# Half of the input transposes as DMA transposes, a re-ordered front and two filler groups in a hand-ordered spectral-plus-MLP kernel

## The chip, the core and the metric

The kernel runs on one core of a Trainium2 chip. A core has a matrix engine (PE; its weight loads are listed apart as PEld), three engines for elementwise work (VectorE or DVE, ScalarE or ACT, GpSimd or POOL), a queue engine that issues DMAs (SyncE or SP; ACT issues some too), and 16 DMA engines that carry them out. Each engine runs its own list of instructions strictly in order and waits on semaphores for the others. The metric is the device time of one execution in microseconds (us).

## The reference, cut to what matters

```python
x = A_x                                                       # 2048 x 512
g = sigmoid((x * gate_w).sum(-1))
a = irfft2(rfft2(x) * (w_r + 1j*w_i))                         # over both axes
h = x @ w1 + b1                                               # 2048 x 1792
b = (h * tanh(softplus(h))) @ w2                              # 2048 x 512
out = g * a + (1 - g) * b
```

Both branches read the same x. B_x is not used.

## The kernel before

**Tiles.** The 2048 rows of x are 16 tiles of 128 rows, t = 0 to 15, and four chunks c of four tiles. The 1792 columns of the hidden layer are 14 blocks ft.

**The MLP branch.** It wants x with its 512 columns on partitions (xT). For this `tr{t}` (PE, four 128x128 transposes against an identity matrix, L547) writes a PSUM bank, and `evx{t}` (ACT or DVE) copies it into xT. `m{c}_{ft}` is a group of four 128x512 matmuls (L791), `h{c}_{ft}` its Mish activation on ACT (L795), `n{t}_0` the second layer for a tile: 14 matmuls of 128x512 (L818).

**The spectral branch.** It goes through stages of 64 small matmuls each, with a copy out of PSUM after each pair: `bf` (sum and difference of the halves of x's columns, DVE, L560), `p` (L570, with the p matrix RF, loaded by `cRF`) and `ep`, `d` (L584) and `ed`, then eight DMAs `sh` that regroup y1 into In (`sh0_*` need d0 to d7 and ed0 to ed3, `sh1_*` the rest), then `t` (L669, with the tables M, loaded by `ldM0` to `ldM3`) and `et`, the filter on DVE (`p2`, `p1`, `ad`, L682 to L690, eight blocks q), an edge correction `e1`, `e2`, `e3` that needs all blocks, then `it` (L743, all of which need e3), the DMAs `hx`, `id` (L767), `ey` and `ip` (L802). `s` and `o` combine both branches, and `out` stores them.

**The filter matrices.** W_r and W_i come by ten DMAs (`wr0s0` to `wi1s1`), and sixteen copies of 32 partitions by 2064 elements (`wrm...`, `wim...`, L626 to L634) spread them out. `win`, `wrn`, `wc` and `wz` finish them.

**The gate.** `gt0` to `gt15` on DVE (L592) multiply x with gate_w, which `gwl` loads, `gwb` (PE) spreads over partitions and `gwe` copies to SBUF.

**What sets the order.** One string, ORDER, names every task once, as `name:engine:slot`. `place` splits it into one list for each engine, and the slot is the PSUM bank (or temporary buffer) that the task's result takes; a task that takes a bank waits for the last readers of what was in it. `emit` turns dependences into semaphore waits. Nothing is reordered at run time, so a task that waits holds all that stands behind it on its engine. An issuing engine likewise holds the DMAs that stand behind a waiting one.

**What the change touches.** XTP is the number of tiles that PE transposes; a tile above it gets `xt{t}`, one DMA from x in HBM to xT with `transpose=True`, issued by SP (L462, L530). NWARM is the number of 128x256 matmuls on a constant that PE runs before x has arrived (`warm`, L488). FILL gives the sizes of groups `fl{k}` of 128x128 matmuls on a constant (L498), whose result is never read. `tab` (L505) is a one-element Mish activation.

Of the kernel before, what the change touches and what calls it, by code (L numbers as in the profile page):

```python
# [301 lines left out]
w1_0:sp x4:sp w1_4:sp x8:sp warm:pe:0 tr0:pe:0 tr1:pe:1 tr2:pe:2 w1_9:sp  # L302
x12:sp wr0s2:sp wi1s1:sp wr1s1:sp wr1s0:sp cFD:sp wr0s0:sp bf0_1:dve bf0_0:dve
evx0:dve wi1s0:sp wr0s1:sp wi0s2:sp wi0s1:sp wi0s0:sp bf2_1:dve ldM1:sp tr3:pe:0
gwb:pe:3 evx1:act bf2_0:dve evx2:act p2:pe:4 p3:pe p0:pe:6 tr_b:pe:2 evx3:dve
gwe:dve p1:pe ep0:act ep2:act ev_b:dve m0_0:pe:2 h0_0:act m0_2:pe:6 m0_1:pe:7
# [7 lines left out]
p13:pe p15:pe gt9:dve gt10:dve ep14:act p8:pe:6 m0_13:pe:4 tr14:pe:5 p9:pe
ep12:act gt11:dve m0_12:pe:0 ep8:act gt12:dve evx14:dve h0_12:act tr12:pe:5 tr13:pe:2
evx12:dve evx13:dve h0_13:act m0_10:pe:3 d4:pe:0 d5:pe ed2:act m1_10:pe:2 h1_10:act
d6:pe:4 d12:pe:6 d13:pe ed6:act d7:pe d14:pe:0 h0_10:act d15:pe m1_13:pe:2
h1_13:act d0:pe:6 d1:pe ed0:act gt13:dve wrm110:dve ed3:dve m0_7:pe:3 d2:pe:4
d3:pe ed1:act m1_12:pe:2 m0_5:pe:6 sh0_2:sp sh0_1:sp ed7:act h0_5:act tr15:pe:4
evx15:act m0_11:pe:5 gt14:dve gt15:dve sh0_0:sp wip1:pool wip0:pool h0_11:act wim010:dve  # L320
# [36 lines left out]
ip0:pe:0 s15_384:dve ip2:pe:2 s2:dve out3:act s13_0:dve s0:dve out13:sp out15_384:sp
out1:act n10_0:pe:5 s10_0:dve s11_0:dve out11:act n15_0:pe:0 s15_0:dve out15_0:act
"""


def _build(nc, A_x, A_w_r, A_w_i, B_x, B_w1, B_b1, B_w2, gate_w, out, XTP=16, LATE=8, NWARM=14,
           W1P=((0, 4), (4, 9), (9, 14)), XP=((0, 2), (2, 4), (4, 8), (8, 12), (12, 16)), SH=2):
    cs = _build_consts()
    d_front = nc.inline_tensor(_bf16_bits(cs["front"]), name="c_front").bitcast(BF)
# [7 lines left out]
    with es:  # L373
        def sb(name, shape, dt):
            return es.enter_context(nc.sbuf_tensor(name, shape, dt))
# [116 lines left out]
        def filler(k, n):  # L492
            fb = _Buf("b1")

            def f_fill(e):
                ins = None
                for _ in range(n):
                    ins = e.matmul(bank(fb)[:, 0:128], one, one, start=True, stop=True)  # L498
                return ins

            G.add(f"fl{k}", "fill", dict(pe=f_fill), ("pe", n, 128), writes=[fb])

        for k_, n_ in enumerate(FILL):
            filler(k_, n_)
# [86 lines left out]
        for t in range(NT):  # L591
            t_gt.append(dve(f"gt{t}", "gate", "stt", 512, lambda e, t=t: e.scalar_tensor_tensor(  # L592
                out=junk, in0=x_sb[:, t, :], scalar=1.0, in1=gwr, op0=ALU.mult, op1=ALU.mult, accum_out=zc[:, t:t + 1]), lock=True,
# [21 lines left out]
        for ri, (dstv, nm) in enumerate(((Wr, "wr"), (Wi, "wi"))):  # L615
            dp = t_bf + t_tr[:XTP] + t_gt if ri else []
            sv = wsr if ri == 0 else wsi
            for fh in range(2):
# [33 lines left out]
                else:  # L652
                    dve(f"{nm}n{fh}", "wm", "dup", 4160, f_dup, lock=True, reads=mv, writes=[wk])
                G.add(f"{nm}c{fh}", "wm", {g: (lambda e, sv=sv, dstv=dstv, f0=f0: e.tensor_copy(
                    out=sv[:, :, f0:f0 + 32].rearrange("p c f -> p f c"), in_=dstv[:, f0:f0 + 32, 0:129:128])) for g in ("dve",)}, ("wc", 64),
# [192 lines left out]
def bass_gated_mix__spectral_gfnet__dense_activation_mish__prompt_kernel(  # L848
    nc: bass.Bass,
    A_x: bass.AP,  # L850
    A_w_r: bass.AP,
    A_w_i: bass.AP,
    B_x: bass.AP,
    B_w1: bass.AP,
    B_b1: bass.AP,
    B_w2: bass.AP,
    gate_w: bass.AP,
    out: bass.AP,
):
    _build(nc, A_x, A_w_r, A_w_i, B_x, B_w1, B_b1, B_w2, gate_w, out)  # L860
# [28 lines left out]
```

## Time and profile before

| | us |
|---|---|
| median of 3 runs | 134.41 (133.45 to 135.21) |
| the profiled execution | 133.68 |
| its span in the profile | 132.4 |
| PE busy / DVE busy / ACT busy in the span | 126.2 / 96.8 / 71.2 |

The profiled execution is longer than its span by 1.3 us, which lie around the program. A PE instruction in the profile is shown from its start to its modelled end, so neighbours overlap: what one takes from the path is the distance between starts, which the chain of waits shows (four 128x128 matmuls in 0.22 us, four of 128x512 in 0.86 us). In a row of the profile, `out<-in` are the names of the SBUF tensors: rA holds x and later W_i, rB the output of bf and later the table G, rX holds xT and later the output, rE holds In, rF the tables M, rS the raw W rows, `ps` is PSUM.

### The profile page before, as it was taken

The numbers are of one execution on the slowest core, as the hardware profiler recorded it, in microseconds if no ns is written. First come the engines' busy times: TensorE is split into PE (matmuls) and PEld (weight loads), VectorE is DVE, ScalarE is ACT, GpSimd is POOL, SyncE is SP. The second block draws the span as 40 slices with busy tenths as digits, with TensorE's granted clock in tenths as the row PEclk, the third lists the DMA queues.
The fourth block names the chain that finished last, engine by engine and source line by source line (L and its number), as shares of the span: only waits on it lengthen the run. The fifth ranks groups of instructions, "written<-read, shape, count | busy, mean of one in ns | idle before, by whom it ended". The sixth has DMA issues, their size and how long they took to land.

```text
span 132.4 us, 2194 instructions
## 1 busy us (share of the span) xinstructions
PE 126.2 (95%) x871; PEld 69.5 (52%) x886; DVE 96.8 (73%) x171; ACT 71.2 (54%) x104; POOL 7.4 (6%) x12
## 2 busy tenths in 40 slices
PE   7796999999999999999999999999999999999992
PEld 5453755766644544655444556744555555455451
DVE  0697898767499999999999616770099597947872
ACT  3469898999979696998770285302122312230000
POOL 3000000000200970000000000000000000000000
PEclk9999999999999999999999999999999999999999
DMA  3799999960387879993397000009800000201463
GB/s 114 227 330 404 219 195 190 202 155 7 139 287 215 236 242 229 269 351 106 87 309 282 0 0 0 5 0 335 309 0 0 5 0 0 79 0 45 161 248 109
DMA packets 12392, 20.16 MB, mean 152 GB/s; under 512 B 1437, under 2 KB 7326, under 8 KB 12318
## 3 DMA queue, kind: packets, MB, share of 16 engines
q1 hardware_dynamic: 11056, 18.05, 47.8%
q10 hardware_dynamic: 1326, 1.97, 4.1%
q8 instruction: 7, 0.11, 0.4%
q14 instruction: 3, 0.02, 0.1%
HBM read 12.66 MB, written 2.10 MB: 111 GB/s over the span
## 4 chain that ended last, share of the span: by engine, by line
PE 89%; DMA 3%; ACT 2%; DVE 2%; issue 1%; SPq 0%
PE ps L818 36%; PE ps L791 34%; DMA rA<-in_A_x_dram 3%; PE ps L570 3%; PE ps L669 3%; PE ps L743 3%; PE ps L584 3%; PE ps L767 3%; PE ps L547 3%; PE ps L802 2%; DVE rX L812 2%; ACT L795 1%; ACT rC L475 1%; ACT hs L795 1%; SPq L463 0%
## 5 line engine op out<-in xcount | busy, mean ns | idle before, releaser
L791 PE MATMUL ps<-rX,w_sb 128*128 128x512 bf16 x216 | 52.2, 379 | 0.6
L791 PEld LDWEIGHTS ps<-rX,w_sb 128*128 128x128 bf16 x224 | 20.4, 98 | 20.5 <-ACT rC L475 0.9
L818 PE MATMUL ps<-w_sb,hs 128*128 128x512 bf16 x109 | 24.7, 379 | 0.2
L795 ACT ACTIVATE hs<-ps,b1f 128x512 bf16<-128x512 f32 x28 | 18.2, 697 | 3.0 <-PE ps L791 2.8
L777 DVE TENSOR_TENSOR rA<-tmp,ps 128x512 bf16<-128x512 f32 x16 | 10.4, 682 | 11.4 <-ACT tmp L475 11.3
L818 PEld LDWEIGHTS ps<-w_sb,hs 128*128 128x128 bf16 x112 | 10.8, 98 | 12.4
L475 ACT ACTIVATE rC<-ps 128x1024 bf16<-128x1024 f32 x13 | 13.0, 1026 | 2.4 <-PE ps L669 1.2
L795 ACT ACTIVATE rS<-ps,b1f 128x512 bf16<-128x512 f32 x14 | 9.3, 699 | 7.2 <-PE ps L791 6.9
L818 PE MATMUL ps<-w_sb,rS 128*128 128x512 bf16 (+2 forms) x68 | 12.7, 335 | 0.1
L818 PE MATMUL ps<-w_sb,rD 128*128 128x512 bf16 x56 | 12.7, 379 | 0.0
L592 DVE SCALAR_TENSOR_TENSOR w_sb<-rA,w_sb 128x512 bf16<-128x512 bf16 x16 | 11.0, 688 | 0.3
L682 DVE TENSOR_TENSOR tmp<-rC,rA 64x1024 bf16<-64x1024 bf16 x16 | 10.6, 684 | 0.4
L795 ACT ACTIVATE rD<-ps,b1f 128x512 bf16<-128x512 f32 x14 | 9.2, 697 | 1.5 <-PE ps L791 1.5
L818 PEld LDWEIGHTS ps<-w_sb,rS 128*128 128x128 bf16 x70 | 6.2, 98 | 5.5
L818 PEld LDWEIGHTS ps<-w_sb,rD 128*128 128x128 bf16 x56 | 5.4, 97 | 6.5 <-DVE rX L808 0.2
L560 DVE TENSOR_TENSOR rB<-rA 128x1024 bf16<-128x1024 bf16 (+1 forms) x10 | 5.4, 578 | 4.5 <-DMA rA<-in_A_x_dram 4.5
L812 DVE SCALAR_TENSOR_TENSOR rX<-ps,omg,rX 128x512 bf16<-128x512 f32 (+2 forms) x9 | 6.1, 687 | 3.0 <-PE ps L818 2.9
L807 ACT ACTIVATE rX<-ps,omg 128x512 bf16<-128x512 f32 x5 | 3.5, 691 | 8.7 <-PE ps L818 8.7
L475 ACT ACTIVATE tmp<-ps 128x512 f32<-128x512 f32 x5 | 2.9, 594 | 9.7 <-PE ps L767 9.7
L547 PE MATMUL ps<-identt,rA 128*128 128x128 bf16 x64 | 5.5, 222 | 2.0 <-ACT omg L505 1.1
L475 ACT ACTIVATE rD<-ps 128x1024 bf16<-128x1024 f32 x7 | 7.1, 1025 | 0.3 <-PE ps L584 0.2
L475 DVE CAST rF<-ps 128x1024 bf16<-128x1024 f32 x5 | 5.8, 1218 | 1.2 <-PE ps L743 1.0
(72 smaller groups left out, 134.4 us busy)
## 6 DMA issues: line engine op xcount, KB each, us to landing
w_sb<-in_B_w_dram SPq DMA_DIRECT2D x4, 640.0 KB, 8.4
rF<-c_m SPq DMA_DIRECT2D x4, 512.0 KB, 5.2
rE<-rD SPq DMA_DIRECT2D x8, 256.0 KB, 3.5
rB<-c_g SPq DMA_DIRECT2D x4, 512.0 KB, 6.2
rC<-rF SPq DMA_DIRECT2D x7, 256.0 KB, 3.0
rA<-in_A_x_dram SPq DMA_DIRECT2D x3, 512.0 KB, 9.7
out_dram<-rX ACTq DMA_DIRECT2D x6, 256.0 KB, 2.1
rW<-rW SPq DMA_DIRECT2D x4, 260.0 KB, 3.5
```

The lines of the kernel that those rows point to most:

```text
L475: fns = dict(dve=lambda e: e.tensor_copy(out=o(), in_=i()), act=lambda e: e.activation(o(), i(), AF.Copy))
L547: ins = e.transpose(bankb(b)[:, 128 * dt_:128 * (dt_ + 1)], x_sb[:, t, 128 * dt_:128 * (dt_ + 1)], identt[:, :])
L560: return e.tensor_tensor(out=xu[:, a:b_, uv, :], in0=x_sb[:, a:b_, 0:256], in1=x_sb[:, a:b_, 256:512], op=ALU.add if uv == 0 else ALU.subt ...
L570: ins = e.matmul(bank(b, i)[:, 128 * c:128 * (c + 1)], xu[:, t, c // 2, c % 2:256:2], RF, start=True, stop=True)
L584: ins = e.matmul(o[:, 2 * e_:2 * e_ + 2, uv, :], zu[:, c, g, :], FD[:, c, :].rearrange("p (r k) -> p r k", r=2), start=True, stop=True)
L592: t_gt.append(dve(f"gt{t}", "gate", "stt", 512, lambda e, t=t: e.scalar_tensor_tensor(out=junk, in0=x_sb[:, t, :], scalar=1.0, in1=gwr, op ...
L682: return e.tensor_tensor(out=zv(z)[lo], in0=Y[hi, f0:f0 + 8, :], in1=Wi[hi, f0:f0 + 8, 0:128], op=ALU.mult)
L777: return e.tensor_tensor(out=yb[:, t:t + 2, 256 * h:256 * h + 256].rearrange("p t (i e) -> p t i e", e=2), in0=t4(z), in1=o4(bank(b, 1)), ...
L791: ins = e.matmul(bank(b), w1_sb[:, dt_, 128 * ft:128 * (ft + 1)], xT[:, c, dt_, :, :], start=(dt_ == 0), stop=(dt_ == 3))
L795: G.add(f"h{c}_{ft}", "mish", dict(act=lambda e, c=c, ft=ft, b=b: e.activation(hs[c][:, ft, :], bank(b), AF.Mish, bias=b1f[:, ft:ft + 1])) ...
L812: dve(name, "fin", "psums", hi - lo, lambda e: e.scalar_tensor_tensor(out=bs[:, t, lo:hi], in0=bank(b)[:, 0:hi - lo], scalar=col[:, t:t + ...
L818: ins = e.matmul(bank(b)[:, 0:hi - lo], hs[c][:, ft, 128 * tl:128 * (tl + 1)], w2_sb[:, ft, lo:hi], start=(ft == 0), stop=(ft == NFT - 1))
```

## The change

The code of the tasks stays; three numbers and the order string change.

```diff
-FILL = ()
+FILL = (3, 9, )
 ORDER = """
-cRF:act braw:act ebase:pool ones:pool ident:pool wrp0:pool x0:sp x2:sp gwl:act
+wrp1:pool ones:pool gwl:act x0:sp wrp0:pool ident:pool warm:pe:0 tr0:pe:0 tr1:pe:1
...
-def _build(..., XTP=16, LATE=8, NWARM=14,
+def _build(..., XTP=8, LATE=8, NWARM=13,
```

With XTP=8, `tr8` to `tr15` and `evx8` to `evx15` are gone, and `xt8` to `xt15` take their place on SP's queue. The new order moves nearly every task. What the prediction speaks of:

**SP's queue after the last piece of x.** Before, these rows follow it: all ten W loads, the d matrix (`cFD`, c_front) and one M table.

```order
L463 DMA rS<-in_A_w_r_dram 16x257
L463 DMA rS<-in_A_w_i_dram 16x32x257
L463 DMA rS<-in_A_w_r_dram 16x32x257
L463 DMA rS<-in_A_w_r_dram 16x8224
L463 DMA w_sb<-c_front 128x512
L463 DMA rS<-in_A_w_r_dram 16x8224
L463 DMA rS<-in_A_w_i_dram 16x8224
L463 DMA rS<-in_A_w_r_dram 16x31x257
L463 DMA rS<-in_A_w_i_dram 16x257
L463 DMA rS<-in_A_w_i_dram 16x31x257
L463 DMA rS<-in_A_w_i_dram 16x8224
L463 DMA rF<-c_m 128x2048
```

In the changed kernel the same place holds three W_r pieces, two M tables, cFD and the eight transposes; behind them come `sh0_*` (rE<-rD x4) and the W_i pieces.

```order
L463 DMA rS<-in_A_w_r_dram 16x8224
L463 DMA rF<-c_m 128x2048
L463 DMA rS<-in_A_w_r_dram 16x257
L463 DMA w_sb<-c_front 128x512
L463 DMA rS<-in_A_w_r_dram 16x31x257
L463 DMA rF<-c_m 128x2048
L462 DMA_TRANSPOSE rX<-in_A_x_dram 128x4x128 x8
L463 DMA rE<-rD 128x1x1024 x4
L463 DMA rS<-in_A_w_i_dram 16x8224
L463 DMA rE<-rD 128x1x1024
L463 DMA rS<-in_A_w_i_dram 16x32x257
L463 DMA rS<-in_A_w_i_dram 16x257
```

So seven of the ten W pieces moved from ahead of the sh DMAs to behind the first of them.

**ACT from its start.** Before: the load of the p matrix (c_front) first, two table loads, the second one at the first Mish (L795), and the one-element Mish (L505) behind that.

```order
L463 DMA w_sb<-c_front 128x128
L463 DMA w_sb<-in_B_b_dram 14x128
L463 DMA w_sb<-in_gate_w_dram 1x512
L475 ACT_TABLE_LOAD
L475 ACTIVATE rX<-ps 128x4x128 x2
L475 ACTIVATE rC<-ps 128x64x16 x2
L795 ACT_TABLE_LOAD
L795 ACTIVATE hs<-ps,b1f 128x512
L505 ACTIVATE omg<-const-float32-1.0 128x1
```

In the changed kernel:

```order
L463 DMA w_sb<-in_gate_w_dram 1x512
L463 DMA w_sb<-in_B_b_dram 14x128
L463 DMA w_sb<-c_front 128x128
L505 ACT_TABLE_LOAD
L505 ACTIVATE omg<-const-float32-1.0 128x1
L475 ACTIVATE rX<-ps 128x4x128 x3
L795 ACTIVATE hs<-ps,b1f 128x512
```

The one-element Mish stands first, the only table load is at it, and the p matrix is the third DMA.

**PE around the edge correction e1 (L702, L703).** Before:

```order
L669 MATMUL ps<-rE,rF 128x128 x8
L791 MATMUL ps<-rX,w_sb 128x512 x24
L818 MATMUL ps<-w_sb,hs 128x512 x28
L702 MATMUL ps<-rC,rD 128x1
L703 MATMUL ps<-rC,rD 128x63
```

In the changed kernel:

```order
L791 MATMUL ps<-rX,w_sb 128x512 x16
L818 MATMUL ps<-w_sb,hs 128x512 x14
L669 MATMUL ps<-rE,rF 128x128 x16
L818 MATMUL ps<-w_sb,hs 128x512 x42
L702 MATMUL ps<-rC,rD 128x1
```

Two tiles of the second layer stood ahead of e1, now four do; three groups of the first layer are left behind it in both.

More of the change, by code (lines that the diff above doesn't have):

```diff
@@ L295, in emit @@
                 eobj.wait_ge(out_sem, 16 * n_out)
-FILL = ()
+FILL = (3, 9, )
 ORDER = """
-cRF:act braw:act ebase:pool ones:pool ident:pool wrp0:pool x0:sp x2:sp gwl:act
[L302 to L306, printed above, removed]
@@ L314 @@
[L314 to L320, printed above, removed]
@@ L357 @@
-ip0:pe:0 s15_384:dve ip2:pe:2 s2:dve out3:act s13_0:dve s0:dve out13:sp out15_384:sp
-out1:act n10_0:pe:5 s10_0:dve s11_0:dve out11:act n15_0:pe:0 s15_0:dve out15_0:act
+wrp1:pool ones:pool gwl:act x0:sp wrp0:pool ident:pool warm:pe:0 tr0:pe:0 tr1:pe:1
+x2:sp fl0:pe:2 tr2:pe:2 braw:act cRF:act tab:act evx0:act w1_0:sp x4:sp
+w1_4:sp bf0_0:dve bf0_1:dve bf2_1:dve bf2_0:dve x8:sp w1_9:sp x12:sp evx2:act
+evx1:act wr0s0:sp ldM0:sp tr3:pe:0 evx3:dve p0:pe:4 p2:pe:6 p3:pe p1:pe
+ep0:dve ep2:dve wr0s2:sp cFD:sp wr0s1:sp ldM1:sp tr_b:pe:0 fl1:pe:3 m0_1:pe:1
@@ new lines @@
+m0_0:pe:4 tr7:pe:5 m0_2:pe:6 ev_b:dve tr6:pe:0 h0_0:act evx7:act h0_2:act tr5:pe:4
+bf4_1:dve bf4_0:dve m0_3:pe:7 h0_1:act h0_3:act evx6:dve tr4:pe:5 evx4:dve gwb:pe:6
+evx5:dve xt8:sp xt9:sp p4:pe:0 p5:pe m0_5:pe:2 gwe:act xt10:sp xt11:sp
+bf8_1:dve ep4:dve bf8_0:dve p6:pe:4 m1_5:pe:3 p7:pe ep6:act h1_5:act xt12:sp
+xt13:sp xt14:sp xt15:sp m1_2:pe:0 m1_6:pe:1 h1_6:act h1_2:act p8:pe:4 p9:pe
+m1_4:pe:3 p10:pe:6 h1_4:act h0_5:act ep8:act m0_11:pe:0 p11:pe m0_8:pe:1 bf12_1:dve
+bf12_0:dve p14:pe:2 p15:pe p12:pe:4 p13:pe h0_8:act ep14:act ep10:dve m0_4:pe:6
@@ new lines @@
+m1_13:pe:1 gt0:dve ep12:dve gt1:dve d4:pe:2 d12:pe:4 h1_13:act h0_4:act d5:pe
+ed2:dve h0_11:act m0_7:pe:7 d13:pe h0_7:act ed6:act m0_9:pe:6 h0_9:act m0_13:pe:2
+d6:pe:0 gt2:dve wrm011:dve gt3:dve d7:pe ed3:dve gt4:dve d0:pe:4 d2:pe:6
+d3:pe m0_10:pe:3 gt5:dve gt6:dve wrm010:dve gt7:dve gt8:dve gt9:dve d1:pe
+h0_13:act ed1:act ed0:act m1_1:pe:2 h1_1:act sh0_2:sp sh0_3:sp sh0_0:sp sh0_1:sp
+m0_6:pe:6 d8:pe:0 h0_6:act h0_10:act m1_10:pe:2 h1_10:act d9:pe m1_9:pe:6 h1_9:act
+gt10:dve ed4:dve d10:pe:2 m1_3:pe:4 d11:pe h1_3:act ed5:act m0_12:pe:6 d14:pe:4
@@ new lines @@
+d15:pe ed7:dve wrm000:act m1_8:pe:7 m1_0:pe:0 t3_0:pe:2 wi0s0:sp t3_1:pe m1_12:pe:1
+t0_0:pe:4 t0_1:pe h1_0:act h0_12:act h1_8:act et0:act h1_12:act m2_12:pe:6 m1_11:pe:7
+t2_0:pe:4 t2_1:pe et3:dve gt11:dve gt12:dve gt13:dve gt14:dve et2:act sh1_0:sp
+wi1s1:sp wi0s2:sp wi0s1:sp gt15:dve wip0:pool wip1:pool h1_11:act m2_5:pe:1 t1_0:pe:2
+t1_1:pe et1:act m2_0:pe:0 m1_7:pe:7 h1_7:act wim000:act zcl:dve m2_2:pe:2 sh1_2:sp
+sh1_3:sp sh1_1:sp h2_2:act h2_0:act m2_6:pe:3 m2_11:pe:7 m2_1:pe:4 m3_2:pe:2 h2_11:act
```

78 lines of the change are left out of this document (34 added, 44 removed).

## The prediction

> **What bounds the kernel now.** The page comes first: the busy line, and the chain that ended last, by engine.
>
> ```profile
> PE 126.2 (95%) x871; PEld 69.5 (52%) x886; DVE 96.8 (73%) x171; ACT 71.2 (54%) x104; POOL 7.4 (6%) x12
> PE 89%; DMA 3%; ACT 2%; DVE 2%; issue 1%; SPq 0%
> ```
>
> PE sets the end, so the question is which PE work goes and where PE waits. The chain in order of time (start, us, what) and the list of waits show where it does:
>
> ```profile
> 5.62 0.62 PE ps L547 x8
> ...
> 7.45 0.34 PE ps L570 x4
> 7.84 0.90 issue
> ...
> 9.77 1.28 ACT L795
> 11.06 0.69 ACT hs L795
> 11.90 0.38 PE ps L547 x4
> ...
> 13.14 0.22 PE ps L547 x4
> ...
> 32.82 1.73 PE ps L791 x8
> ...
> 76.23 3.02 PE ps L818 x14
> ...
> 130.07 0.62 DVE rX L812
> PE ps L547 <- ACT omg L505: 1.1, 1, 1.1
> PE ps L547 <- DMA rA<-in_A_x_dram: 0.9, 1, 0.9
> ```
>
> Up to 11.9 us PE waits twice for named things: 0.9 us for x2, and 1.1 us behind ACT, where the table load at the first Mish (1.28) delays the activation that frees a bank. Behind 11.9 the chain is PE nearly throughout. One more place is tight, seen in the timeline where DVE ends the filter and PE starts e1:
>
> ```profile
> 72.87 0.69 DVE L690 TENSOR_TENSOR rC<-rC,tmp 128x1024 bf16<-128x1024 bf16 x1
> 73.96 0.17 PE L702 MATMUL ps<-rC,rD 128*128 128x1 bf16 x1
> ```
>
> The filter ends at 73.56, and e1 follows at once: DVE and PE arrive together, so an order that loses DVE time ahead of e1 loses it for PE.
>
> **Part by part.**
>
> *Transposes off PE.* 32 matmuls go; four take 0.22 us of the chain (13.14): 8 x 0.22 = **-1.8**, all on the path.
>
> *Warm-up, 13 instead of 14.* tr0 waits for x0 either way: 0.
>
> *Table load early.* It runs while ACT waits for tr0, and the 1.1 us wait goes. What is late next is x4, which tr7 (PE's ninth group) wants. When x4 lands is bounded by the windows (us, PE, PEld, DVE, ACT, POOL, clock, DMA share, GB/s) and by its first reader (bf4 at 10.40; bf12, the reader of x12, at 19.21):
>
> ```profile
> 0.00:5.00 5.00, 3.86 (x22) 2.45 (x22) 1.03 (x3) 1.53 (x2) 1.05 (x8) 1.00 0.40 123
> 5.00:10.00 5.00, 4.18 (x35) 2.36 (x37) 4.17 (x13) 3.11 (x5) 0.00 (x0) 1.00 0.98 326
> 10.00:15.00 5.00, 3.90 (x34) 2.25 (x33) 3.44 (x10) 4.61 (x9) 0.00 (x0) 1.00 1.07 352
> 15.00:20.00 5.00, 4.95 (x45) 3.03 (x45) 4.93 (x11) 4.71 (x8) 0.00 (x0) 1.00 1.21 187
> 10.40 1.29 DVE L560 TENSOR_TENSOR rB<-rA 128x1024 bf16<-128x1024 bf16 x2
> 19.21 1.29 DVE L560 TENSOR_TENSOR rB<-rA 128x1024 bf16<-128x1024 bf16 x2
> ```
>
> x0, x2, w1_0 and x4 are 1.57 MB; 0.62 MB move by 5 us, the rest at 326 GB/s takes 2.9: 7.9 at the earliest, 10.4 at the latest. PE itself is ready for tr7 at about 9.6 (p ends at 7.8 now, gwb's 0.3 leaves that place, nine fillers of 0.06 and two groups of 0.86 come). So PE runs dense from 9.6 to 10.4 on, I take 9.9. At 11.9, where it does so now, one more group (0.86) and gwb (0.2) were done, so the gain is 11.9 - 9.9 - 1.1 = **-0.9** (-0.4 to -1.2).
>
> *Fillers.* At 0.22/4 each, three cost 0.17 inside the 0.9 us wait for x2: 0. Nine cost 0.5 ahead of the first group m0_1, which also needs w1_0, 1.05 MB into the queue: 0.62 MB by 5 us and 1.3 us more, 6.3 at the earliest. Where it lands behind the fillers, they are free: **+0.1** (0 to 0.5).
>
> *p matrix as ACT's third load.*
>
> ```profile
> 1.97 0.25 ACTq L463 DMA_DIRECT2D w_sb<-in_gate_w_dram  x1
> 6.17 0.38 PE L534 MATMUL ps<-w_sb,const-bfloat16-1.0 1*128 1x512 bf16 x1
> w_sb<-c_front ACTq DMA_DIRECT2D x1, 32.0 KB, 2.9
> ```
>
> Issued at 1.97 instead of first, it lands at 4.9; what is issued there now was used at 6.17, and p0 comes at 6.1 at the earliest: 0 (0 to 0.1).
>
> *The transposes on SP and the DMA engines.* The trace has none. Ahead of them stand the x and W1 pieces (3.93 MB; 4.0 MB have moved by 15 us, and bf12 reads x12 at 19.2 at the latest: 17 taken), three W_r pieces (0.53 MB at 187 GB/s, 2.8) and two M tables with cFD (1.2 MB at 340, 3.5): 23.3. Lower bound for each, 128 KB at 340 GB/s: 0.4 us. Upper, a small load of 256-byte rows that nothing overlaps, the 2.9 of the p matrix. I take 0.7 (128 KB at the 187 GB/s of the window in which W's 514-byte rows move; the nearest in row length): 8 x 0.7 = 5.6, so they end at 29. The Trainium skill ("DMA: Bandwidth & Descriptors", Latency and other measured facts) gives 261 GB/s for a DMA transpose, by an estimate 0.5 us each and the end at 27.3, with the same sum; no run here shows it yet.
>
> They matter through sh0 behind them:
>
> ```profile
> 33.91 2.79 SPq L463 DMA_DIRECT2D rE<-rD  x4
> 43.27 0.39 PE L669 MATMUL ps<-rE,rF 128*128 128x128 bf16 x4
> rE<-rD SPq DMA_DIRECT2D x8, 256.0 KB, 3.5
> ```
>
> Now the first t comes 9.4 us after the first sh0. In the new order, from 9.9 on, d1 stands behind 15 groups of the first layer, 12 p, 10 d, 4 tr and gwb: 15 x 0.86 + 26 x 0.22 + 0.2 = 18.8, at 28.7, ed0 and ed1 follow on ACT, 31. t3_0 stands behind 8 more groups and 6 d, at 37. Four issues (2.8) and a landing (3.5) bring sh0 in at 36.6 if SP is free at 31. With 29 it is: **0**, with 0.4 us in hand. The first xT that comes by DMA is read by m2_12 behind 38.
>
> *DVE up to e1.* Two more second-layer tiles (6.04) stand ahead of e1, so PE reaches it at 73.96 + 6.0 - 1.8 - 0.9 + 0.1 = 77.4. DVE's work moved behind x12:
>
> ```profile
> L592 DVE SCALAR_TENSOR_TENSOR w_sb<-rA,w_sb 128x512 bf16<-128x512 bf16 x16 | 11.0, 688 | 0.3
> L592 DVE DVE_READ_ACCUMULATOR w_sb<-rA,w_sb 128x1 f32 x16 | 1.3, 82 | 0.0
> L682 DVE TENSOR_TENSOR tmp<-rC,rA 64x1024 bf16<-64x1024 bf16 x16 | 10.6, 684 | 0.4
> L687 DVE TENSOR_TENSOR rC<-rC,rW 128x1024 bf16<-128x1024 bf16 x8 | 5.3, 689 | 0.2
> L690 DVE TENSOR_TENSOR rC<-rC,tmp 128x1024 bf16<-128x1024 bf16 x8 | 5.5, 692 | 0.2
> L634 DVE TENSOR_SCALAR rW<-rS 32x2064 bf16<-32x2064 bf16 x4 | 2.8, 699 | 0.1
> L643 DVE TENSOR_SCALAR rA<-rA 64x4160 bf16<-64x4160 bf16 x2 | 2.4, 1232 | 0.1
> L475 DVE CAST rC<-ps 128x1024 bf16<-128x1024 f32 x3 | 3.7, 1249 | 0.4 <-PE ps L570 0.4
> L654 DVE COPY wsi<-rA 128x64 bf16<-128x64 bf16 x2 | 0.7, 325 | 0.1
> ```
>
> From bf12 on it has 1.3 (bf) + 12.3 (gate) + 7 x 1.25 + 13 x 0.70 + 2.4 + 21.4 (filter) + 1.8 (four of L654 and the small ones) = 57. From x12 (17, at most 19.2) it ends at 74 to 76.2: 1.2 to 3.4 us of slack. **0.**
>
> *W_i late.* DVE wants wi0s1 behind 23.9 of the 57, at 41 to 43. It is issued behind sh1_0, which waits for ed7: d15 at 35.2, copied at 37, three more issues, then 256 KB and two pieces at 187 GB/s, about 43. Inside the slack, but close: **+0.3** (0 to 2).
>
> *ACT takes three W copies*, at 2064 elements.
>
> ```profile
> L475 ACT ACTIVATE rC<-ps 128x1024 bf16<-128x1024 f32 x13 | 13.0, 1026 | 2.4 <-PE ps L669 1.2 <-PE ps L570 1.2
> L475 ACT ACTIVATE rX<-ps 128x512 bf16<-128x512 bf16 x9 | 5.3, 602 | 2.0 <-PE ps L547 1.9
> ```
>
> 512 more elements take 0.42, so one takes 1.03 + 2.03 x 0.42 = 1.9. Behind it the activations stand that free PE's banks, while PE fills one in 0.86 us. Bounds: 0, and 3 x (1.9 - 0.7) = 3.6. I take **+0.8**, less than one bank's time in all.
>
> *Tail.* 128 columns are now last instead of 384, about **-0.1**.
>
> Sum: -1.8 - 0.9 + 0.1 + 0.3 + 0.8 - 0.1 = -1.6 on the 133.68 of the profiled execution, 132.1. That execution lies 0.73 below the median of 134.41; runs to come are measured like the median, so the forecast is **132.8**. This measurement tells about 2% from no change: below 131.7 or above 137.1.
>
> **The rivals.**
>
> *Faster.* The ACT copies hide and x4 is early: -1.8 - 1.2 - 0.1 = -3.1, **131.3**. For it: the chain behind 11.9 has hardly a wait today, with a tighter DVE. Against: both need the friendly end of a bound.
>
> ```profile
> rS<-in_A_w_i_dram SPq DMA_DIRECT2D x3, 257.0 KB, 12.5
> ```
>
> *Slower: the transposes hold SP.* One after another, each from issue to landing. Past (31 + 0.4 - 23.3)/8 = 1.0 us each, sh0 is late and t3_0 stops PE. At 1.5 each they end at 35.3: +3.9, 136.7; at 2.9, +15.1, 147.9. For it: eight DMAs ahead of the tightest transfer, a price known to a factor of seven. Against: the W pieces (row above) are issued 12.5 us ahead of their landing, so SP can run ahead of the data. Worse still, a tile's four blocks could go in turn, each at 0.7 to 2.9; from 2.8 for a tile on the time is 147 and more. The Trainium skill ("VectorE: DVE Perf Modes", The three transpose paths) speaks against the change: 1309 ns by DMA for a 128x128 block against 390 on PE, with the advice to use PE; no run shows it here. By an estimate from it, 1.3 for a whole tile gives 135.1, four blocks in turn 166.
>
> *Slower: W_i.* If wi0s1 takes 12.5 us to land as now, it comes at 51 instead of 43: 8 less a slack of 2.3 is +5.7, **138.5**. Against: now it stands behind nine pieces, then behind three DMAs.
>
> *No gain.* The change moves PE's work forward only to meet DVE at e1: if the slack is gone by 1.6 us, 134.4.
>
> **How the numbers follow.** Forecast 0.40. Faster 0.22. Transposes 0.25, of which 0.07 stay within 2% (under 1.5 us each) and 0.04 are the four blocks in turn. W_i 0.10. No gain 0.03. Faster by over 2%: 0.22; within: 0.40 + 0.07 + 0.03 = 0.50; slower: 0.18 + 0.10 = 0.28. The range leaves out about 0.1 at each end: from 130.6 (the faster case with 0.7 to spare) to 140 (above W_i, transposes at 1.9). The likeliest case's own is 131.8 to 134.5.
>
> **What would show it.** No wait of PE on ACT L505; PE dense from about 10 us. Transposes done by 29, sh0 issued near 31, no stop ahead of the first L669. e1 near 77 to 78, and DVE's L690 done before it. If PE waits at the first L669 behind In, the second rival holds; if DVE idles at L634 behind the W_i rows, the third.

## The result, and the profile after

| | before | changed | ratio (95%) |
|---|---|---|---|
| first set, 20 runs of each | 133.88 (133.36 to 135.93) | 132.47 (131.22 to 136.79) | 0.985 (0.982 to 0.988) |
| second set, beside experiments | 133.18 (133.02 to 134.62) | 132.15 (131.86 to 132.57) | 0.991 (0.987 to 0.994) |

The changed kernel is about 1.2% faster, within the 2% called no change. As the same kernel gave 0.985 and 0.991 in two sets, experiments are compared inside one set wherever they can be. Ratios leave out executions more than 1.5% above the fastest of their kernel, as the profiled one of the first set (133.89) is; the lines below are of the second profiled execution (c_after, 132.03, span 130.6) unless said otherwise.

The busy line, and the chain by engine:

```profile
PE 126.3 (97%) x865; PEld 69.8 (53%) x865; DVE 97.9 (75%) x166; ACT 69.7 (53%) x98; POOL 6.0 (5%) x14
PE 86%; DMA 7%; SPq 4%; DVE 1%; issue 1%
```

PE is as busy as before in a span that is 1.8 us shorter. The chain now also passes through the load of the third M table and SP's queue ahead of it (DMA 7%, SPq 4%). In PE's list of waits (total, times, longest) these two are new:

```profile
PE ps L791 <- ACT rD L795: 0.8, 1, 0.8
PE ps L669 <- DMA rF<-c_m: 0.6, 1, 0.6
```

The first is for Mish results that go into rD (held by the late `sh1_*`, which read rD), the second for the third M table. The 1.1 us behind ACT L505 are gone. The timeline, first PE at tr7, then SP (the eight transposes in one row, then the first three of them singly), then PE where the forecast had its two check points, and DVE at e1:

```profile
9.57 0.39 PE L547 MATMUL ps<-identt,rA 128*128 128x128 bf16 x4
...
10.67 17.97 SPq L462 DMA_TRANSPOSE rX<-in_A_x_dram  x8
10.67 5.25 SPq L462 DMA_TRANSPOSE rX<-in_A_x_dram  x1
15.97 3.95 SPq L462 DMA_TRANSPOSE rX<-in_A_x_dram  x1
19.96 1.27 SPq L462 DMA_TRANSPOSE rX<-in_A_x_dram  x1
30.04 2.59 SPq L463 DMA_DIRECT2D rE<-rD  x4
...
37.04 0.61 PE L669 MATMUL ps<-rE,rF 128*128 128x128 bf16 x8
...
77.76 0.69 DVE L690 TENSOR_TENSOR rC<-rC,tmp 128x1024 bf16<-128x1024 bf16 x1
78.50 0.10 PEld L702 LDWEIGHTS ps<-rC,rD 128*128 128x128 bf16 x1 [0.20 <-DVE rC L690]
78.63 0.17 PE L702 MATMUL ps<-rC,rD 128*128 128x1 bf16 x1
```

SP stands in the eight transposes until 28.64, sh0 goes out at 30.04, the first t comes at 37.04 without a wait: nearly the times of the forecast (29, 31, 37); in the first profile sh0 goes out at 32.1 and the first t comes at 39.1. But eight issues take SP 17.97 where 5.6 was forecast. They are not alike: the first two hold SP for 5.25 and 3.95, until 19.9, the other six for 1.27 to 1.93, 1.45 on average, where 0.7 was forecast. They end in time because SP begins with them at 10.7, not at 23.3. And e1 comes at 78.6 instead of 77.4, with the weight load waiting for DVE.

The ledger against before: e1 is at 78.63 instead of 73.96, +4.67, with 6.04 of second-layer work moved ahead of it: a gain of 1.4. Behind e1 the span is 130.6 - 78.63 = 52.0 against 132.4 - 73.96 - 6.04 = 52.4: 0.4 more. Together 1.8, of which 0.9 is the wait for x2 (0.9 before, none here). That wait is between 0 and 1.1 us in the profiles of this case, 1.1 in the first profile of the changed kernel, so this half of the ledger is luck of the execution.

### The profile page after: what moved, and what is told of

Its sections match the earlier page's. It is cut to its first block, busy times and chain, and to the rows that moved or that the text cites. A ratio compares the mean times of both kernels' runs of the same rounds, so it can differ in the third digit from the quotient of the medians.

```text
span 132.4 us, 2172 instructions
## 1 busy us (share of the span) xinstructions
PE 126.6 (96%) x850; PEld 70.6 (53%) x865; DVE 97.8 (74%) x166; ACT 69.8 (53%) x98; POOL 6.0 (5%) x14
## 4 chain that ended last, share of the span: by engine, by line
PE 79%; DMA 8%; DVE 4%; SPq 3%; ACT 3%; issue 1%; ACTq 0%
PE ps L818 34%; PE ps L791 27%; DMA rE<-rD 5%; DMA rA<-in_A_x_dram 4%; PE ps L570 3%; SPq L463 3%; PE ps L584 3%; ACT rD L795 3%; PE ps L743 3%; PE ps L767 2%; PE ps L802 2%; DVE rX L812 2%; PE ps L669 1%; PE ps L547 1%; DVE rD L475 1%
## 5 line engine op out<-in xcount | busy, mean ns | idle before, releaser
L795 ACT ACTIVATE hs<-ps,b1f 128x512 bf16<-128x512 f32 x28 | 18.0, 685 | 6.6 <-PE ps L791 6.3
L475 ACT ACTIVATE rC<-ps 128x1024 bf16<-128x1024 f32 x10 | 10.1, 1024 | 5.0 <-PE ps L669 2.8
L475 ACT ACTIVATE tmp<-ps 128x512 f32<-128x512 f32 x6 | 3.6, 596 | 14.7 <-PE ps L767 14.7
L475 DVE CAST rC<-ps 128x1024 bf16<-128x1024 f32 x6 | 7.3, 1222 | 5.3 <-PE ps L570 4.4
L795 ACT ACTIVATE rS<-ps,b1f 128x512 bf16<-128x512 f32 x14 | 9.3, 699 | 3.4 <-issue 1.6
L795 ACT ACTIVATE rD<-ps,b1f 128x512 bf16<-128x512 f32 x14 | 8.8, 695 | 0.4 <-DMA rE<-rD 0.4
L808 DVE TENSOR_SCALAR rX<-ps,omg 128x512 bf16<-128x512 f32 x4 | 3.1, 766 | 8.0 <-PE ps L818 8.0
L807 ACT ACTIVATE rX<-ps,omg 128x512 bf16<-128x512 f32 x4 | 2.6, 685 | 11.2 <-DVE omg L599 7.4
L812 DVE SCALAR_TENSOR_TENSOR rX<-ps,gcol,rX 128x512 bf16<-128x512 f32 x8 | 5.9, 746 | 0.6 <-PE ps L802 0.6
```

The source lines that it names most:

```text
L475: fns = dict(dve=lambda e: e.tensor_copy(out=o(), in_=i()), act=lambda e: e.activation(o(), i(), AF.Copy))
L795: G.add(f"h{c}_{ft}", "mish", dict(act=lambda e, c=c, ft=ft, b=b: e.activation(hs[c][:, ft, :], bank(b), AF.Mish, bias=b1f[:, ft:ft + 1])) ...
L812: dve(name, "fin", "psums", hi - lo, lambda e: e.scalar_tensor_tensor(out=bs[:, t, lo:hi], in0=bank(b)[:, 0:hi - lo], scalar=col[:, t:t + ...
```

## The experiments

Ratios are to the kernel before, run on the same chip in the same set. The changed kernel (c_after) was run again only in the set of a_nofill, a_tr and a_split; where another experiment is set beside it, the comparison is across sets, which for the changed kernel itself differ by 0.6%.

### The early table load alone (b_tab)

```diff
 gwl:act
+tab:act
 w1_0:sp
...
 m0_1:pe:7
-tab:act
 h0_1:act
```

> The kernel before with one edit: the one-element Mish moved to ACT's first place, so that the table load lies ahead of the first copy. Theory (the early table load is worth 0.9 us of the front): PE's wait of 1.1 us behind ACT L505 is gone and PE is 0.9 us earlier at 12 us (0.4 to 1.2); the time falls by 0.9 us, ratio 0.993. Rival (DVE sets e1): PE is earlier in the front, but the filter ends at 73.6 all the same and e1 waits for DVE L690; the time falls by 0.4 us at most, ratio 0.997 to 1.000. Second rival (the next wait, for x4, takes its place): nothing changes at 12 us, ratio 1.000.

Measured: 132.36 against 133.56, ratio 0.993 (0.988 to 0.997), 1.0 us. Its list of PE's waits has no ACT L505 any more:

```profile
PE ps L547 <- DMA rA<-in_A_x_dram: 0.2, 1, 0.2
```

The first theory holds in size by the run times. The trace does not show the 0.9 us: the twelve runs fall into two groups, 131.9 to 132.4 and 133.6 to 133.9, and the profiled one (133.58, span 132.3) is of the upper. There tr7 starts at 11.80 against 11.90 before, because the first group of the first layer comes 0.8 later (8.51 against 7.71); the last section says why.

### The transposes alone (b_xt, b_xt4)

All eight, or only the last four, by DMA in the old order, behind SP's last load ahead of sh0.

In b_xt4 it is XTP=12 and xt12 to xt15 alone; `tr` and `evx` of these tiles go.

```diff
-XTP=16
+XTP=8
...
 ldM1:sp
+xt8:sp xt9:sp xt10:sp xt11:sp xt12:sp xt13:sp xt14:sp xt15:sp
```

> The kernel before with one edit: tiles 8 to 15 come by DMA transposes, put on SP behind the last M table ahead of sh0; 32 matmuls and eight copies go. Theory (32 matmuls on the path at 0.22 us for four): 1.8 us less, ratio 0.987, the four copies that leave DVE let the filter end as much earlier. Rival (DVE and sh set the time, not PE): ratio 0.997 to 1.000, with PE waiting ahead of e1 or of the first t. Second rival (a transpose costs SP 2.3 us, 18.44 us for eight in the changed kernel): SP is held to about 36 instead of 34, sh0 comes 2 to 5 us late; there are some 4 us between its landing and the first t, so 0 to 1 of the gain is lost.

> The kernel before with one edit: only tiles 12 to 15 come by DMA transposes, four of them on SP behind the last M table; 16 matmuls and four copies go. SP, free at 20 us there, is held by 4 x 2.2 to about 29, and sh0 goes out near 34 in any case. Theory (a transpose on PE is worth its 0.22 us where SP has the time for the DMA): 0.9 us less, ratio 0.993, and no clock below 0.999. Rival (PE's front or DVE at e1 sets the time, not the transposes): 0.997 to 1.000, with PE waiting at L702 for DVE. Second rival (transposes always cost more than they free): slower, 1.005 and more.

b_xt: 137.44 against 133.56, slower by 2.9% at the median and by 0.8% in its best run (134.67 to 139.94); its runs lie too far apart for a ratio. Its timeline, SP and then PE:

```profile
19.34 17.44 SPq L462 DMA_TRANSPOSE rX<-in_A_x_dram  x8
36.91 2.58 SPq L463 DMA_DIRECT2D rE<-rD  x4
...
38.50 1.86 PE L791 MATMUL ps<-rX,w_sb 128*128 128x512 bf16 x4 [3.78 <-DMA rX<-in_A_x_dram]
```

And its windows around the stop (length, PE busy, granted clock, DMA share, GB/s):

```profile
36.00:38.00 2.00, 0.00 (x0) 1.00 0.51 114
38.00:40.00 2.00, 1.50 (x4) 0.60 0.92 342
```

All three expectations were wrong on the place: sh0 did go out 3.0 us later (36.91 against 33.91), but PE never waits for it; it waits for the transposed tiles themselves, which the old order reads at 34.7. The eight take SP 2.2 us each on average, as expected, though singly from 1.27 to 4.62, and starting at 19.3 that isn't hidden. After the stop the row of four matmuls of 128x512 shows 1.86 where such a row shows 1.03 elsewhere: the granted clock is 0.60.

b_xt4: 133.08 against 133.47, ratio 0.997 (0.994 to 1.000), a gain of 0.4 where 0.9 was expected. Behind the W rows four issues hold SP for 13.13, singly 1.89 to 4.74, in its timeline:

```profile
19.51 13.13 SPq L462 DMA_TRANSPOSE rX<-in_A_x_dram  x4
33.74 2.67 SPq L463 DMA_DIRECT2D rE<-rD  x4
```

and PE's list of waits has two that before had not:

```profile
PE ps L791 <- DMA rX<-in_A_x_dram: 0.6, 1, 0.6
PE ps L584 <- ACT hs L795: 0.5, 1, 0.5
```

sh0 still goes out at its old time (33.74 against 33.91). In this execution (133.70, above the median) the waits of 0.6 and 0.5 take what the 16 matmuls freed: e1 comes at 73.97, as before.

### Four more transposes in the changed kernel (a_xt4)

```diff
 xt15:sp
+xd0:sp xd1:sp xd2:sp xd3:sp
```

`xd` reads a tile of x like `xt` and writes it into the part of rF that `ldM2` loads later.

> The changed kernel with four more DMA transposes on SP behind the eight, into a part of the M tables that is loaded later; nothing reads them. Theory A (what a transpose costs is SP's own time, 18.44 us for eight = 2.3 us each, and it is hidden only because SP starts on them at 10.4 us): SP is free at 38.1 instead of 28.9, sh0 goes out 6.0 us later than 32.1, of which 2.0 us are in hand at the first t; PE stops there for 4 us and the time rises by about 4 us, ratio to the kernel before 1.015 to 1.02. Theory B (the cost is the DMA engines' time, 0.5 to 0.65 us between landings): SP is free by 31.5, sh0 goes out as before, the time stays, ratio 0.985.

Measured: 139.65, ratio 1.047 (1.040 to 1.054). SP's timeline, the four together and then the first of them alone (its lines are one lower here, the first t is L672):

```profile
28.54 9.42 SPq L463 DMA_TRANSPOSE rF<-in_A_x_dram  x4
28.54 1.27 SPq L463 DMA_TRANSPOSE rF<-in_A_x_dram  x1
38.07 2.58 SPq L464 DMA_DIRECT2D rE<-rD  x4
```

SP's wait between them, PE's wait at the first t, and the windows behind that:

```profile
SPq L463 <- DMA rF<-in_A_x_dram: 4.5, 3, 1.6
PE ps L672 <- DMA rE<-rD: 5.4, 1, 5.4
```

```profile
42.00:44.00 2.00, 1.28 (x10) 0.50 0.98 264
44.00:46.00 2.00, 2.00 (x12) 0.50 1.03 181
46.00:48.00 2.00, 2.00 (x9) 0.58 1.21 154
```

sh0 goes out at 38.07, as theory A had it (38.1), but not for its reason. The four issues take 1.27, 1.19, 1.19 and 1.19, and between them SP waits 4.5 us for landings: all four `xd` are entered as writers of the same part of rF, so each waits until the one ahead of it has landed. That 4.84 of issues and 4.5 of waits come near 4 x 2.2 is chance, and the experiment does not separate the two theories. What it does show is what a late sh0 costs. The time rose by more than the 4 us expected: PE stops for 5.4, and at half clock from 42.7 to about 47.5 (0.50, 0.50, 0.58) it loses another 2.5 or so.

### Tiles 8 to 15 back on PE (a_tr), and the changed kernel again (c_after)

Four of the copies are on ACT and four on DVE; c_after is the changed kernel without an edit.

```diff
-XTP=8
+XTP=16
...
-xt8:sp xt9:sp xt10:sp xt11:sp
...
-xt12:sp xt13:sp xt14:sp xt15:sp
...
 m0_9:pe:6 h0_9:act
+tr8:pe:3 evx8:act
...
 gt5:dve
+tr9:pe:0 evx9:dve
...
 m0_12:pe:6
+tr15:pe:1 evx15:dve
```

> The changed kernel with tiles 8 to 15 transposed by PE again (32 matmuls, four copies on ACT and four on DVE, put where a PSUM bank stands free between 19 and 31 us), everything else in the new order. Theory (32 matmuls on the path at 0.22 us for four): 1.8 us more than the changed kernel, ratio to the kernel before 0.998. Rival (the DMA transposes are worth nothing, the gain is the front's): no difference, 0.985. Second rival (SP held by transposes stops PE in some executions, seen as a granted clock of 0.987 in 4 of 20): with the transposes gone no execution shows a clock below 0.999, and the time is 0.5 to 1.5 us more at the fast end but the slow ones go.

> The changed kernel once more, unaltered, to stand beside the three that follow and to get a profile of another execution. Ratio to the kernel before 0.985 as measured. Theory (the phase of PE's start decides the first 10 us): where PE's 128x128 matmuls of the front stand 0.055 us apart instead of 0.107 as in the first profile, the first L791 group starts near 7.6 instead of 10.1. Theory (late sh1 is a lasting cost): the waits on ACT rD L795, 0.4 and 0.85 us, are seen again; rival: they belonged to that execution alone.

a_tr: 135.77, ratio 1.017 (1.012 to 1.022), against 0.991 for c_after in the same set: 3.5 us, twice what was expected. At the first t it is 2.96 us behind c_after (40.00 against 37.04), at e1 3.35 (81.98 against 78.63), in the timeline and the list of PE's waits:

```profile
40.00 0.61 PE L669 MATMUL ps<-rE,rF 128*128 128x128 bf16 x8
...
81.98 0.10 PEld L702 LDWEIGHTS ps<-rC,rD 128*128 128x128 bf16 x1 [0.51 <-DVE rC L690]
```

```profile
PE ps L791 <- ACT rD L795: 1.6, 1, 1.6
PE ps L584 <- ACT hs L795: 0.7, 2, 0.4
```

The 32 matmuls explain 1.8 by their count. Ahead of the first t PE also waits 0.7 for ACT and loses some 0.8 in gaps that the list does not name, less 0.4 by which its front is earlier; behind it sh1 goes out 3.1 us later and what follows is late with it. That this comes with the eight copies and the places chosen for them is likely, but not shown. So in this order the DMA transposes save 3.5 us against this one way of doing without them, 1.8 of it by the matmuls' count, and the front is not the whole gain. In this form the new order is 1.7% slower than the kernel before although it has the early table load: the rest of the re-ordering does not pay by itself. One of its six runs had a granted clock of 0.988 with no DMA transpose in the program, so the second rival falls too. c_after had one of the two waits for rD again (0.8), and 0.6 for an M table; a_crf below has 1.0 and 0.7, a_nofill neither. The front of c_after is 2.3 us earlier than in the first profile (first group at 7.85 against 10.12), as the first theory of c_after had it.

### The fillers (a_nofill)

```diff
-FILL = (3, 9, )
+FILL = ()
```

> The changed kernel without its two filler groups. Theory (nine of the twelve stand on the path, 9 x 0.055 = 0.5 us): 0.5 us less than the changed kernel, ratio to the kernel before 0.981. Rival (the prediction's own 0.1 us): no difference. Second rival (the fillers keep PE's rate up through the wait for x2): the 128x128 matmuls of the front stand 0.107 us apart up to about 10 us in more of the executions; 0.5 to 1.5 us more, ratio 0.989 to 0.996.

Measured: 131.32 (131.03 to 131.74) against 132.15 (131.86 to 132.57) for the changed kernel in the same set; no run of the one reaches the other. Ratio 0.983 (0.979 to 0.987). PE's front, of c_after and then of this kernel:

```profile
5.80 1.47 PE L570 MATMUL ps<-w_sb,rB 128*128 128x128 bf16 x16
...
7.31 0.70 PE L498 MATMUL ps<-const-bfloat16-1.0 128*128 128x128 bf16 x9
7.85 1.89 PE L791 MATMUL ps<-rX,w_sb 128*128 128x512 bf16 x8
```

```profile
7.03 1.04 PE L791 MATMUL ps<-rX,w_sb 128*128 128x512 bf16 x4
8.31 1.04 PE L791 MATMUL ps<-rX,w_sb 128*128 128x512 bf16 x4 [0.24 <-DVE rC L475]
9.27 0.40 PE L547 MATMUL ps<-identt,rA 128*128 128x128 bf16 x4
```

The first group starts 0.82 us earlier: nine fillers take 0.54 there, and the three ahead of tr2 hide behind nothing when x2 is in time. That this is also the whole difference (0.83) is chance. The second group waits for DVE, and at tr7 only 0.30 is left (9.27 against 9.57), as it still is at the first t. At e1 the lead is 0.88 (77.75 against 78.63), because PE's waits for rD and the M table are not there, and with them goes a wait of DVE that stands in c_after's list:

```profile
DVE tmp L682 <- ACT rC L475: 0.5, 1, 0.5
```

So in these two profiles 0.3 is the front and about 0.5 these waits. Neither run without fillers (a_best below is the other) has them, and c_after, a_crf and a_wdve all have them; how the fillers would bring them about is not shown. The second rival falls: the first three fillers kept no rate up.

### The order of the small loads (a_crf)

```diff
+cRF:act braw:act gwl:act
 wrp1:pool ones:pool
-gwl:act
...
-braw:act cRF:act
 tab:act
```

> The changed kernel with ACT's small loads in the order of the kernel before: the p matrix first, the bias, then gate_w. Theory (the prediction's 0: p0 comes behind x2, not behind the p matrix): no difference to the changed kernel, ratio to the kernel before 0.988 to 0.991. Rival (the small loads ahead of the p matrix delay it to 6.4 us and with it p0): 0.4 us less, 0.986. Second rival (they shift x0 and x2 in the queue): x2 is used earlier or later by as much as the time changes.

Measured: 132.10, ratio 0.992 (0.989 to 0.995), the same as the changed kernel in the other two sets (0.985 and 0.991) as far as those agree: nothing is seen, and 0 was forecast.

### ACT's three W copies (a_wdve)

```diff
-wrm000:act
+wrm000:dve
...
-wim000:act
+wim000:dve
...
-wrm100:act
+wrm100:dve
```

> The changed kernel with ACT's three W copies (1.9 us each) back on DVE (0.7 each). Theory A (DVE sets e1: its last L690 ends 0.2 us ahead of PE's L702, which waits for it): DVE gets 2.1 us more ahead of e1 and loses a wait of 0.6 behind ACT; 1.5 us more than the changed kernel, ratio to the kernel before 1.000. Theory B (the prediction's 0.8 us: the copies on ACT hold up the activations that free PE's banks): 0.8 us less, ratio 0.985.

Measured: 132.66, ratio 0.993 (0.991 to 0.996), beside 0.992 for a_crf in its set, which stands for the changed kernel there: 0.2 us, inside the uncertainty. Neither theory holds in size: moving the copies off ACT gains nothing, and 2.1 us more on DVE cost far less than the 1.5 expected. DVE loses its wait of 0.6 behind ACT L631 and reaches its second L643 0.7 later than in c_after (58.96 against 58.23). The wait of 0.5 behind ACT L475 that c_after has later on falls away and makes up for most of that: e1 comes at 78.79, where L702 waits 0.55 instead of 0.20.

### SP's queue re-ordered (a_wi, a_split)

SP's queue in a_wi:

```diff
 ldM1:sp
+wi0s0:sp wi0s2:sp wi0s1:sp
 xt8:sp
...
 sh0_1:sp
-wi0s0:sp
 sh1_0:sp
-wi1s1:sp wi0s2:sp wi0s1:sp
 sh1_2:sp sh1_3:sp sh1_1:sp
+wi1s1:sp
```

and in a_split:

```diff
 ldM1:sp
+wi0s0:sp wi0s2:sp wi0s1:sp wi1s1:sp wi1s0:sp
 xt8:sp xt9:sp xt10:sp xt11:sp xt12:sp xt13:sp
-xt14:sp xt15:sp
+ldM2:sp
 sh0_2:sp sh0_3:sp sh0_0:sp sh0_1:sp
-wi0s0:sp
 sh1_0:sp
-wi1s1:sp wi0s2:sp wi0s1:sp
 sh1_2:sp sh1_3:sp sh1_1:sp
+xt14:sp xt15:sp
-wi1s0:sp ldM2:sp
```

> The changed kernel with SP's queue re-ordered: three W_i pieces (0s0, 0s2, 0s1) ahead of the transposes instead of between the sh DMAs, the fourth (1s1) behind the last sh1. Theory (new waits behind late sh1 give back about 1.3 us of the gain): sh1 lands by 43 instead of 49, ACT's Mish into rD at 49 and PE's two waits for it (0.41 and 0.85) go, DVE's wait for W_i (0.81) goes; 0.8 to 1.3 us less than the changed kernel, ratio to the kernel before 0.976 to 0.979. Rival (DVE sets e1): PE runs earlier up to e1 and waits there; 0 to 0.4 us less, ratio 0.982 to 0.985. Second rival (SP is held longer ahead of sh0 by the three issues, 2.0 us of the 3.2 it has in hand, and the transposes land 2 to 3 us later): as far as that reaches the first t, slower than the changed kernel, ratio 0.985 to 0.995.

> The changed kernel with SP's queue re-ordered further: all five W_i pieces ahead of the transposes, six transposes and the third M table ahead of sh0, the last two transposes behind the last sh1. Theory (SP ends its transposes at 28.9 us against 32.1 where sh0 can go, which leaves too little for executions in which they run late, and sh1 stands behind W_i): SP is free near 27.5 at the latest, sh1 goes out right behind sh0; no execution with a clock below 0.999, no wait on ACT rD L795; ratio to the kernel before 0.975 to 0.980. Rival (the waits for sh1 cost nothing at the end, DVE sets e1): as the changed kernel, 0.983 to 0.986. Second rival (the last two transposes, 4.6 us of SP behind 39, come too late for the third layer of tiles at 48 to 50 and hold PE): 0.99 and more.

a_wi: 132.35 (131.03 to 135.78), ratio 0.986 (0.979 to 0.993), too wide to tell from the changed kernel. The trace tells more. PE's waits for rD and M are gone, as expected, and e1 comes at 78.1, 0.5 us earlier. DVE in c_after, then in a_wi:

```profile
46.93 1.24 DVE L643 TENSOR_SCALAR rA<-rA 64x4160 bf16<-64x4160 bf16 x1 [0.55 <-ACT rA L631]
48.80 0.70 DVE L634 TENSOR_SCALAR rA<-rS 32x2064 bf16<-32x2064 bf16 x1
```

```profile
46.96 1.24 DVE L643 TENSOR_SCALAR rA<-rA 64x4160 bf16<-64x4160 bf16 x1 [1.26 <-ACT rA L631]
48.84 0.70 DVE L634 TENSOR_SCALAR rA<-rS 32x2064 bf16<-32x2064 bf16 x1
...
77.35 0.69 DVE L690 TENSOR_TENSOR rC<-rC,tmp 128x1024 bf16<-128x1024 bf16 x1
78.09 0.10 PEld L702 LDWEIGHTS ps<-rC,rD 128*128 128x128 bf16 x1 [0.49 <-DVE rC L690]
```

W_i is there early, but DVE now waits 1.26 for the copy of it on ACT, and is at L634 at 48.8 as before. Behind that point one wait of DVE is gone, the 0.5 for ACT L475, the copy of a t result that PE's waits had made late, and the last L690 ends at 78.04 against 78.45. PE, freed of 1.4 us of waits, now waits 0.49 at L702. In the changed kernel, then, about 0.4 of PE's waits for sh1 and M reach e1, and the rest lies in the shadow of DVE.

a_split: 138.67 (136.45 to 139.43), ratio 1.023 (1.016 to 1.030) by the two shortest of six runs, 1.041 by the medians; slower than all that was expected.

```profile
10.18 9.29 SPq L463 DMA_DIRECT2D rS<-in_A_w_i_dram  x5
19.52 13.04 SPq L462 DMA_TRANSPOSE rX<-in_A_x_dram  x6
...
33.31 6.55 SPq L463 DMA_DIRECT2D rE<-rD  x8
39.90 3.15 SPq L462 DMA_TRANSPOSE rX<-in_A_x_dram  x2
...
40.60 1.01 PE L669 MATMUL ps<-rE,rF 128*128 128x128 bf16 x8 [3.32 <-DMA rE<-rD]
```

The arithmetic behind the expectation took 0.6 us for a W_i issue; five took 9.29, the last two 2.78 and 4.17. SP is held until 19.5 there, about as long as by the first two transposes in c_after (19.9), whichever loads stand in that place. The trace of the kernel before had shown that W rows can hold SP, two for 4.21:

```profile
8.31 4.21 SPq L463 DMA_DIRECT2D rS<-in_A_w_r_dram  x2
```

In a_split SP is free at 33.2 instead of 27.5, sh0 goes out 3.3 us later than in c_after (30.04), and PE stops for 3.3 us and goes on at half clock. So what the rival feared does happen, a queue that holds SP beyond sh0's time, but with plain loads in part of it; the count had left out 5.7 us of SP's time.

### The best version that was tried (a_best)

No fillers, and xt15 moved into SP's idle time between sh0 and sh1.

```diff
-FILL = (3, 9, )
+FILL = ()
...
 xt14:sp
-xt15:sp
...
 wi0s0:sp
+xt15:sp
```

> The changed kernel without its fillers, and with the last transpose moved from ahead of sh0 to behind it, into SP's idle time ahead of sh1. Theory (SP ends its transposes 1 us ahead of sh0 and is late in some executions): the median as without fillers, ratio 0.983, and no execution over 1% above the median, none with a clock below 0.999. Rival (DVE sets e1, which waits 0.5 us for it there): the same median. Second rival (the third layer of tiles now waits for its last tile): PE waits at L791 for rX at 47 us, ratio 0.99.

Measured: 131.26 (130.81 to 132.68), ratio 0.986 (0.982 to 0.990), beside 0.983 (0.979 to 0.987) for a_nofill in its own set: moving xt15 shows no effect on the median, and the spread is not smaller (the longest run is 1.1% above the median). Alone behind sh0 the issue takes SP 1.27 us. The version to keep is the changed kernel without fillers, the simpler of the two; it is faster than both kernels.

## Why the prediction was right, point by point

| step | forecast | measured |
|---|---|---|
| time | 132.8 (130.6 to 140.0) | 132.47; 132.15 in the second set |
| gain | 1.6 | 1.4; 1.0 in the second set |
| sum for a profiled execution | 132.1 | 133.89 (first), 132.03 (c_after) |
| transposes off PE | -1.8 | -3.5 with all that hangs on them (a_tr); b_xt4 -0.4 for half of them |
| early table load | -0.9 | -1.0 by run times (b_tab) |
| fillers | +0.1 (0 to 0.5) | +0.8 (a_nofill), of which 0.3 is seen at tr7 |
| small loads | 0 | none seen (a_crf) |
| one transpose on SP | 0.7, from 23.3 on | 5.25 and 3.95 for the first two, from 10.7 on, then 1.27 to 1.93 |
| SP free, sh0 out, first t | 29, 31, 37 | 28.6, 30.0, 37.0 (first profile 28.9, 32.1, 39.1) |
| e1 | 77.4, DVE 1.2 to 3.4 us ahead | 78.6, DVE 0.2 us behind |
| ACT's W copies | +0.8 (0 to 3.6) | no gain from moving them back, 0.2 the other way (a_wdve) |

**The front** was right as a mechanism. x4 did not become the next late thing: in c_after tr7 runs at 9.57, right when PE reaches it. The price of the fillers was wrong: "where it lands behind the fillers, they are free" assumed w1_0 or x2 late, and both were in time in c_after (in the first profile x2 was 1.1 us late).

**The transposes on SP** were right in the result, and the mechanism only in outline. The forecast had two stages: the loads ahead until 23.3, then eight transposes at 0.7, to 28.9. The trace has two stages too: SP issues the first transpose at 10.7 and is held in the first two until 19.9, about as long as by plain loads in their place (19.5 in a_split); from then on it needs 1.45 for each of the six that are left, to 28.6. The price is twice the forecast's, which came from the DMA engines' bandwidth, and the stage starts 3.4 us earlier and with two already issued. That the two errors cancel is luck. The threshold of the slower rival, 1.0 us each, is wrong by the same step: from 19.9 it is (31.4 - 19.9)/6 = 1.9 for each of the six. The rival's outcome is real: a late sh0 costs a_xt4 about 6% and a_split about 3% over the changed kernel. The Trainium skill's rule against the change ("VectorE: DVE Perf Modes", The three transpose paths and Rules for kernel authors: 1309 ns by DMA against 390 on PE, use PE) has a figure for one block that lies nearer to SP's price for a tile of four blocks than the forecast did: 1.27 for the one that was issued alone. It does not decide the time here, since SP has 18 us to spare that PE has not.

**DVE up to e1** is the term that was mis-sized. It was given 1.2 to 3.4 us of slack; in every profile of the new order L702 waits 0.2 to 0.55 for its last L690. The count had the work right and left out the waits. x12 is read at 16.99 in c_after, as taken, and from there to e1 the windows show DVE (length, busy):

```profile
17.00:40.00 23.00, 19.44 (x36) 1.00 0.78 164
40.00:60.00 20.00, 17.80 (x32) 1.00 1.07 270
60.00:79.00 19.00, 17.75 (x33) 1.00 0.49 136
```

It is busy 55.0 of 62 us where 57 were counted, and its rows there name PE, ACT and W_i as what it waits for in the other 7. So "W_i late" and "ACT's copies", entered as 0.3 and 0.8 on PE's path, act through DVE instead: W_i holds L634 for 0.8 and ACT's copy of it holds L643 for 0.55, and from 48.8 on DVE has hardly a wait. On PE's side tr7 comes 0.3 earlier than the 9.9 of the forecast, and the three waits behind it (0.8, 0.6, 0.2) make 1.6: together 1.3, and e1 is 1.2 late. Of the first two, a_wi shows that about 0.4 would be won back and DVE holds the rest. a_wi has W_i early but leaves its copy on ACT, a_wdve moves the copy but leaves W_i late; the two together, or another order for DVE, were not tried.

**The sum** fits better than its terms. e1 is 1.2 us later than the forecast's 77.4, which the 1.1 that was entered apart for W_i and ACT nearly covers, and behind e1 0.4 is gained instead of 0.1. That 132.03 meets 132.1 is luck in part: the sum starts from an execution with 0.9 us of wait for x2 and is met by one with none, while the first profiled execution took 133.89. The median forecast started from a median of three runs (134.41) that the later sets put at 133.88 and 133.18. What is borne out is the size of the gain, 1.0 to 1.4 against 1.6, the front, and that sh0 is not held; what the transposes alone are worth in the old order is not, since b_xt lost and b_xt4 gained 0.4.

## What to carry to other kernels

A DMA has two prices, that of the data and that of its issue, and they are paid at different places: read the issuing queue's rows for the second, one issue at a time, since a row that joins several hides how unlike they are. Start the count where the queue is free, and look there for issues that it is held in. When an engine "has slack" up to a meeting point, count its waits with its work, since a small wait elsewhere reaches the end through it. A filler is free only where the wait that it fills is really there in most executions.

## What the runs showed of the hardware that was not expected

- **An issue holds SP for a time that depends on its place.** A DMA transpose of 128x512 takes SP 1.27 us alone (a_best), 1.19 to 1.27 where each waits for the landing of the one ahead (a_xt4), but 5.25 and 3.95 for the first two behind the loads of c_after. Plain W loads do the same: 2.78 and 4.17 in a_split, where others take 0.6. That SP is held by a queue still full of what stands ahead fits all of these; no run separates it from other causes.
- **A stop of PE costs more than itself.** After stops of 3.3 to 5.4 us the profile's granted clock is 0.50 to 0.60 over the 4 to 6 us of windows behind them (0.60 and 0.55 in b_xt, 0.60 and 0.54 in a_split, 0.50, 0.50 and 0.58 in a_xt4).
- **PE's first microseconds run at half rate for a time that varies**, with the granted clock shown as 1.00. In the first profile of the changed kernel 128x128 matmuls are 0.107 us apart up to 10 us, and a wait for x2 lies in between:

```profile
6.10 1.04 PE L547 MATMUL ps<-identt,rA 128*128 128x128 bf16 x8 [1.06 <-DMA rA<-in_A_x_dram]
6.93 1.92 PE L570 MATMUL ps<-w_sb,rB 128*128 128x128 bf16 x16
```

  In c_after the 16 matmuls of L570 take 1.47, in a_wi 1.06, and the rate is full from about 6 us on. The Trainium skill ("TensorE: Matmul & The Clock Gate", Part 1: The HAM clock gate) says that the array starts at half rate and is released after a busy window of about 3.4 us that is not aligned to the kernel. The rows agree that the length varies; at some 9 us in the first profile (0.8 to 10) it is more than one such window, and why is not shown. It gives the two groups of b_tab's runs, 1.5 us apart, a cause that fits (the profiled run of the upper group has L570 at half rate), but no run of the lower group was profiled. It also fits a_best, whose profiled execution is the longest of its six (132.68) and has L570 at 1.91.
